# Attention over a memory, then a squared-ReLU MLP: two batches alternate in six pieces instead of four, and each state read runs three batches behind its scores

## The chip, the core and the metric

The kernel runs on one core of a Trainium2 chip. The core has a matrix engine (PE, with its weight loads PEld), a vector engine (DVE), an activation engine (ACT), a general engine (POOL) and a queue engine (SP). Each takes its own instructions in a fixed order, and they meet at semaphores. SP issues nearly all DMAs here, ACT a few. The metric is the time of the program on the device in microseconds (us): before, the median of three runs is 734.01 us (733.97 to 734.39).

## The reference

There are B = 8 batches with H = 8 heads, S = 512 rows of x and N = 32 rows of state per head, each row D = 64 wide. Attention goes both ways between x and state, and the rows of both pass through one MLP:

```python
a  = softmax(x @ state.T / 8);   xread = a  @ state    # 512 rows a batch
a2 = softmax(state @ x.T / 8);   sread = a2 @ x        # 32 rows a batch
rows = concat([xread, sread])    # heads side by side: 544 x 512 a batch
out  = relu(rows @ w_in)**2 @ w_out                    # 512 -> 2048 -> 512
```

Both weight matrices arrive as 8-byte floating point words.

## The kernel before, in words

**Precision.** A matrix product in full precision is made of three products of shortened operands: each operand is cut by `split` (lines 95 to 97) into a high part (a cast on ACT, L96) and a low part (a subtraction on DVE or POOL, L97). The first few products use whole operands instead (`PLAIN_Z`, `PLAIN_X`).

**Weights.** Every weight tile is brought from 8-byte words to single precision by `singles` (L106 to L116): one ACT instruction and four DVE instructions on 128x512. There are 16 tiles of `w_in` (`wf<-w_raw`) and 16 of `w_out` (`wof<-wo_raw`), so 128 such DVE instructions. The converted `w_in` is also stored to DRAM (`wd`), since the second half of the states and the state rows need it again.

**Products with the state.** `xread @ w_in` is never built from `xread`: per head, z = state @ w_in is computed once for a group of four batches (`z_part`, group 0 from the fresh weights, group 1 later from `wd`), copied from PSUM by ACT (`z_stage`, L199) and stored to DRAM (`zd`). `z_fetch` brings the rows of one batch back and splits them (`z_hi`, `z_lo`).

**The units of work.** `mlp` runs over chunks `fc` of 128 of the 2048 hidden columns. A unit is one chunk for one batch: six products into `ph` (the up product, L377), ReLU on ACT (L379), the square (on ACT for the first ten units, then on DVE, L383), the split into `g_hi` (ACT) and `g_lo` (DVE), and twelve products into four accumulators `po` (the down product, L403), two units later. The eight batches have 128 units of 18 products of 128x512; 16 units of 256 columns for the state rows follow at the end. `BOTH` says in which pieces batches 0 and 1 take turns, so that a weight chunk serves two batches while the next is prepared. At the end of a piece the four accumulators are emptied by `rows`.

**Attention.** For each batch and each half of its heads: `scores` (which leaves `e2` and its sum for the state side), `soft1` and `soft1b` (the softmax for the x side, ending in `a_hi`, `a_lo`), and the state read: `load_n`, `cut_n` (split of x, `xn_hl`), `turn` (transposes of `e2` into `e_hl`) and `read` (products `pr`, summed into `sr`).

**What sets the order.** Two lists of steps, `weights` and `reads`, are emitted between units by due times. After that the tile framework's scheduler reorders the instructions of each engine by its own estimates, so the engines' orders have to be read from the built program. They are static: on the chip an instruction that waits holds up all that stands behind it on its engine.

**Buffers.** Tiles of one tag share a number of buffers: `raw` (4) holds weight words, the raw state of group 1 (`st_raw`) and the partial sums on their way back (`so_far`); `x_hl` (1) holds the split x; `xraw` (2) the raw x.

Of the kernel before, what the change touches and what calls it, by code (L numbers as in the profile page):

```python
# [18 lines left out]
def memory_attention_then_relu2_ffn(  # L19
# [19 lines left out]


    nc = tc.nc
    P = 128
# [22 lines left out]
    PLAIN_X = 2  # L65
    BOTH = ((0, 2), (1, 6), (0, NFC), (1, NFC))
    READS = (14, 28)

# [53 lines left out]
    def z_state(G):  # L122
        if G == 0:
            raw = const.tile([P, H, GB * N], F32, name="st_f")
            st["raw"] = raw
        else:
            raw = sb.tile([P, H, GB * N], F32, name="st_raw", tag="raw", bufs=RAW)
        src = stT.rearrange("d (h b n) -> d h b n", h=H, b=B)[:, :, G * GB:(G + 1) * GB, :]
        for j in range(2):
            nc.sync.dma_start(  # L130
                out=raw[j * D:(j + 1) * D].rearrange("d h (b n) -> d h b n", b=GB), in_=src
            )
        hi = sb.tile([P, H, GB * N], F32R, name="stz_hi", bufs=1)
        lo = sb.tile([P, H, GB * N], F32R, name="stz_lo", bufs=1)
        split(hi, lo, raw, nc.gpsimd)
        st[G] = hi, lo

    def z_part(G, k, g):
# [36 lines left out]
        def product(i):  # L175
            def run():
# [65 lines left out]
    def attention_group(b, g, pair):  # L242
# [25 lines left out]
        def scores():  # L268
# [96 lines left out]

    def mlp(width, fcs, first, rows, aux, at_end=None):

# [39 lines left out]
        for i in range(len(fcs) + 2):  # L407
            if i <= last:
                up(fcs[i])
                aux()  # L410
            elif i == last + 1 and at_end:
                at_end()
            if i >= 2:
# [7 lines left out]

    def moved(t, po):
        os_ = sb.tile([P, DM], F32, name="os_", bufs=3)
        if t % 2:
            nc.scalar.copy(out=os_, in_=po)
        else:
            nc.vector.tensor_copy(out=os_, in_=po)
        return os_

# [75 lines left out]
    def order(b):  # L505
        _, pad, (p, q) = attentions[b]
        if b == 1:
            return [
                pad, p["load_t"], p["cut_t"], q["load_t"], p["scores"], p["soft1"], q["cut_t"],
                q["scores"], p["soft1b"], q["soft1"], q["soft1b"],  # L510
            ]
        return [
            pad, p["load_t"], p["cut_t"], q["load_t"], p["scores"], p["soft1"], q["cut_t"],
            p["soft1b"], p["load_n"], q["scores"], q["soft1"], p["turn"], p["cut_n"], q["load_n"],
            q["soft1b"], p["read"], q["cut_n"], q["turn"], q["read"],
        ]
# [17 lines left out]
    for m in range(NFC):  # L534
# [10 lines left out]
        weights.add(steps, 2 * min(at[m], at[m - m % FPC] - 2))  # L545
    weights.add([lambda: z_state(1), z1[0][0], z1[0][2], z1[1][0]], 2 * ends[0] + 4, 2 * ends[0])
    for m in range(NFC):
# [3 lines left out]
        if m + 2 < NFC:  # L551
            steps.append(z1[m + 2][0])
        due = 2 * (ends[0] + (begins[GB] - ends[0]) * (m + 1) // (NFC + 1))
        weights.add(steps, due, 2 * ends[0])
# [10 lines left out]

    half_sums = {}
    for b, fcs in parts:
# [16 lines left out]

        whole = fcs[0] == 0
        so_far = []

        def fetch(b=b, so_far=so_far):
            for t in range(0, NT, 2):
                so_far.append(sb.tile([P, 2, DM], F32, name="so_far", tag="raw", bufs=RAW))  # L590
                nc.sync.dma_start(out=so_far[-1], in_=half_sums[b][:, t:t + 2, :])

        def rows(t, po, b=b, fcs=fcs, so_far=so_far):
            if so_far:
                total = so_far[t // 2][:, t % 2, :]
                nc.vector.tensor_add(out=total, in0=total, in1=po)
            else:
                total = moved(t, po)
            if fcs[-1] < NFC - 1:
                if t == 0:  # L600
                    half_sums[b] = dr.tile([P, NT, DM], F32, name=f"half_{b}_{fcs[0]}")
                nc.sync.dma_start(out=half_sums[b][:, t, :], in_=total)
            else:
                nc.sync.dma_start(out=out[b * R + t * P:b * R + (t + 1) * P, :], in_=total)

        mlp(S, fcs, first, rows, aux, None if whole else fetch)


# [24 lines left out]
    def rows(t, po):  # L633
        tile_ = moved(t, po)
        dst = out.rearrange("(b r) e -> b r e", r=R)[t * GB:(t + 1) * GB, S:R, :]
# [36 lines left out]
```

## Time and profile before

| what | value |
|---|---|
| median of 3 runs | 734.01 us (733.97 to 734.39) |
| the profiled execution's own time | 734.09 us |
| its span, first to last instruction | 732.3 us |
| what lies around the span | 1.8 us |
| PE busy | 684.3 us (93%) |
| DVE busy | 480.5 us (66%) |
| ACT busy | 400.8 us (55%) |
| POOL busy | 229.8 us (31%) |
| moved by DMA | 94.71 MB, 129 GB/s over the span |
| granted PE clock, mean | 0.959 |

The span is the time from the first to the last instruction; the execution's own time has 1.8 us more. Shares over the whole span hide the stages: in the first quarter DVE is at nine tenths and more while PE has gaps, afterwards PE is full. A table by windows of time shows both.

### The profile page before, as it was taken

To read this page: it belongs to the slowest core of one execution; us is meant where nothing else is said; L and a number is where in the kernel's file an instruction comes from. 1 tells how busy PE (TensorE), PEld (TensorE's weight loads), DVE (VectorE), ACT (ScalarE), POOL (GpSimd) and SP (SyncE) were. 2 spreads that over 40 slices of the span, in tenths; PEclk is the share of its full clock that TensorE was granted. 3 is DMA by queue.
4 is the path that set the end of the run, shared out by engine and by line. 5 is a ranking of instruction groups with operands and counts; after the bars stand their busy time and mean duration, and the time that the engine had idled before them with its cause. 6 is when DMAs were issued, how large, how long until landed. Compare 5 with 4: busy or idle time off the path is not lost.

```text
span 732.3 us, 9282 instructions
## 1 busy us (share of the span) xinstructions
PE 684.3 (93%) x3112; PEld 554.6 (76%) x3112; DVE 480.5 (66%) x777; ACT 400.8 (55%) x720; POOL 229.8 (31%) x198
## 2 busy tenths in 40 slices
PE   4978887988999999999999999999999999999994
PEld 1545765766788888878887888888888888888893
DVE  4997999984577496438859688486444445433542
ACT  3667786665587587567546555465333334333441
POOL 2455554556367455432432421421110000000000
PEclk9577988998999999999999999999999999999998
DMA  9879788765543844444212431230021112000420
GB/s 260 272 250 303 258 274 264 216 180 164 179 148 114 248 145 146 132 170 142 90 59 81 141 91 34 86 115 30 29 71 46 35 36 86 30 15 0 144 59 29
DMA packets 74163, 94.71 MB, mean 129 GB/s; under 512 B 3972, under 2 KB 55940, under 8 KB 74116
## 3 DMA queue, kind: packets, MB, share of 16 engines
q1 hardware_dynamic: 56708, 77.34, 33.8%
q10 hardware_dynamic: 17408, 16.78, 6.8%
q8 instruction: 24, 0.39, 0.2%
q14 instruction: 23, 0.19, 0.1%
HBM read 62.13 MB, written 31.98 MB: 129 GB/s over the span
## 4 chain that ended last, share of the span: by engine, by line
PE 75%; DVE 12%; ACT 5%; issue 3%; DMA 3%; SPq 0%; ACTq 0%; DVEq 0%
PE po L403 44%; PE ph L377 24%; PE pr L340 2%; DMA st_f<-stT 1%; DVE wof L112 1%; PE pq L274 1%; DVE wof L107 1%; PE pz L182 1%; DVE z_lo L97 1%; DVE wf L112 1%; DVE wof L116 1%; PE pz L190 1%; PE pz L189 1%; DVE g_lo L97 1%; DVE sp_hl L235 1%
## 5 line engine op out<-in xcount | busy, mean ns | idle before, releaser
L403 PE MATMUL po<-wo_hi,g_hi 128*128 128x512 f32 x544 | 218.8, 404 | 11.3 <-ACT g_hi L96 10.5
L403 PE MATMUL po<-wo_lo,g_hi 128*128 128x512 f32 x544 | 217.9, 402 | 0.0
L383 DVE TENSOR_TENSOR ph<-ph,r 128x512 f32<-128x512 f32 (+1 forms) x134 | 89.1, 665 | 150.8 <-ACT r L379 150.3
L379 ACT ACTIVATE r<-ph 128x512 f32<-128x512 f32 (+1 forms) x144 | 82.5, 574 | 167.8 <-PE ph L377 167.2
L403 PE MATMUL po<-wo_hi,g_lo 128*128 128x512 f32 x544 | 157.0, 400 | 1.4 <-DVE g_lo L97 1.1
L403 PEld LDWEIGHTS po<-wo_hi,g_hi 128*128 128x128 f32 x544 | 104.2, 192 | 36.3 <-ACT g_hi L96 13.2
L97 DVE TENSOR_TENSOR g_lo<-ph,g_hi 128x512 fp32r<-128x512 f32 (+1 forms) x144 | 94.5, 656 | 45.6 <-ACT g_hi L96 36.3
L403 PEld LDWEIGHTS po<-wo_lo,g_hi 128*128 128x128 f32 x544 | 105.0, 193 | 23.1 <-POOL wo_lo L97 0.7
L403 PEld LDWEIGHTS po<-wo_hi,g_lo 128*128 128x128 f32 x544 | 103.0, 192 | 23.4 <-DVE g_lo L97 1.5
L96 ACT CAST g_hi<-ph 128x512 fp32r<-128x512 f32 (+1 forms) x144 | 81.1, 563 | 48.0 <-DVE ph L383 35.5
L377 PE MATMUL ph<-a_hi,z_hi 128*128 128x512 f32 x256 | 83.1, 406 | 6.2 <-DVE g_lo L97 4.8
L171 POOL TENSOR_TENSOR w<-wf,w 64x512 fp32r<-64x512 f32 x52 | 72.4, 1392 | 50.7 <-ACT w L170 34.7
L377 PE MATMUL ph<-a_hi,z_lo 128*128 128x512 f32 x256 | 81.4, 399 | 0.0
L377 PE MATMUL ph<-a_lo,z_hi 128*128 128x512 f32 x256 | 81.1, 396 | 0.0
L97 POOL TENSOR_TENSOR xn_hl<-xn_raw,xn_hl 128x1024 fp32r<-128x1024 f32 x16 | 39.1, 2445 | 94.8 <-ACT xn_hl L96 87.3
L377 PEld LDWEIGHTS ph<-a_hi,z_hi 128*128 128x128 f32 x256 | 47.8, 193 | 18.6 <-DVE g_lo L97 6.5
L377 PEld LDWEIGHTS ph<-a_hi,z_lo 128*128 128x128 f32 x256 | 49.4, 193 | 11.1
L377 PEld LDWEIGHTS ph<-a_lo,z_hi 128*128 128x128 f32 x256 | 48.8, 191 | 11.1
L97 DVE TENSOR_TENSOR z_lo<-z_raw,z_hi 128x512 fp32r<-128x512 f32 x64 | 54.4, 850 | 2.1 <-ACT z_hi L96 2.1
L97 POOL TENSOR_TENSOR xt_hl<-xt_raw,xt_hl 128x1024 fp32r<-128x1024 f32 x12 | 29.2, 2437 | 65.5 <-ACT xt_hl L96 41.0
L96 ACT CAST z_hi<-z_raw 128x512 fp32r<-128x512 f32 x64 | 39.4, 616 | 8.0 <-DMA z_raw<-zd 7.6
L199 ACT COPY z_stage<-pz 128x512 f32<-128x512 f32 x64 | 37.1, 585 | 6.4 <-PE pz L190 4.8
(124 smaller groups left out, 836.0 us busy)
## 6 DMA issues: line engine op xcount, KB each, us to landing
zd<-z_stage ACTq DMA_DIRECT2D x64, 256.0 KB
z_raw<-zd SPq DMA_DIRECT2D x63, 256.0 KB
xt_raw<-xT SPq DMA_DIRECT2D x16, 512.0 KB
w_raw<-w_in SPq DMA_DIRECT2D x16, 512.0 KB
wo_raw<-w_out SPq DMA_DIRECT2D x16, 512.0 KB
xn_raw<-xn SPq DMA_DIRECT2D x16, 512.0 KB
wd<-wf SPq DMA_DIRECT2D x16, 256.0 KB
wf<-wd SPq DMA_DIRECT2D x16, 256.0 KB
```

The source lines that it names most:

```text
L96: nc.scalar.copy(out=hi, in_=src)
L97: eng_lo.tensor_sub(out=lo, in0=src, in1=hi.bitcast(F32))
L107: nc.vector.tensor_scalar_max(out_f, out_f, 2.0**-15)
L112: nc.vector.scalar_tensor_tensor(out=bits, in0=high, scalar=-0x40000000, in1=bits, op0=ALU.bitwise_and, op1=ALU.bitwise_or,)
L116: nc.vector.scalar_tensor_tensor(out=bits, in0=low, scalar=29, in1=bits, op0=ALU.logical_shift_right, op1=ALU.bitwise_or,)
L171: nc.gpsimd.tensor_sub(out=w[other], in0=wf[own], in1=w[own].bitcast(F32))
L199: nc.scalar.copy(out=stage, in_=pz)
L340: nc.tensor.matmul(pr[:, q].rearrange("p i c -> p (i c)"), lhsT=my["e"][:, t, q].rearrange("p i n -> p (i n)"), rhs=my["xn"][:, t, q].rear ...
L377: nc.tensor.matmul(ph, lhsT=w, rhs=v, start=i == 0, stop=i == len(todo) - 1)
L379: nc.scalar.activation(r, ph, AF.Relu)
L383: nc.vector.tensor_mul(out=ph, in0=ph, in1=r)
L403: nc.tensor.matmul(po[t], lhsT=g, rhs=w, start=i == 0 and j == 0, stop=i == last and j == 2)
```

## The change

1. `BOTH` has six pieces. Batch 0 now takes chunks 0-1, 2-9 and 10-15, batch 1 takes 0-5, 6-9 and 10-15. Numbered from 0, the units of batch 0 are 0-1, 8-15 and 20-25, those of batch 1 are 2-7, 16-19 and 26-31 (before: 0-1 and 8-21; 2-7 and 22-31). Due times of the weights follow: chunks 10 to 15 are first needed at units 20 to 25, before at 16 to 21.
2. The partial sums no longer go to DRAM (`half_...`: 8 stores of 256 KB, 4 loads of 512 KB). Each batch has a tile `sum` of 128x4x512 in SBUF; the first piece moves its accumulators there (two on ACT, two on DVE), later pieces add to it on DVE, eight additions more in all.
3. Room for it: `st_f` shares the buffer of `x_hl`, `z_stage` has three buffers instead of four, `os_` goes into `raw`.
4. The steps of a state read (`order_read`) are listed with the scores of the batch three later; the reads of batches 5, 6 and 7 are due at 10, 20 and 30 slots into batch 7 (two slots a unit). `e2` and `s2` have six buffers instead of four.
5. The work on state group 1 is due between units 32 and 64, before between 22 and 64.

```diff
-    BOTH = ((0, 2), (1, 6), (0, NFC), (1, NFC))
-    READS = (14, 28)
+    BOTH = ((0, 2), (1, 6), (0, 10), (1, 10), (0, NFC), (1, NFC))
+    LATE = 3
...
-            raw = const.tile([P, H, GB * N], F32, name="st_f")
+            raw = sb.tile([P, H, GB * N], F32, name="st_f", tag="x_hl", bufs=1)
...
-                stage = sb.tile([P, nq, FW], F32, name="z_stage", bufs=4)
+                stage = sb.tile([P, nq, FW], F32, name="z_stage", bufs=3)
...
-            e2 = sb.tile([P, S], F32, name="e2", bufs=4)
-            s2 = sb.tile([P, 1], F32, name="s2", bufs=4)
+            e2 = sb.tile([P, S], F32, name="e2", bufs=2 * LATE)
+            s2 = sb.tile([P, 1], F32, name="s2", bufs=2 * LATE)
...
-    weights.add([lambda: z_state(1), z1[0][0], z1[0][2], z1[1][0]], 2 * ends[0] + 4, 2 * ends[0])
+    z1_from = begins[GB - 2]
+    weights.add([lambda: z_state(1), z1[0][0], z1[0][2], z1[1][0]], 2 * z1_from + 4, 2 * z1_from)
...
-    reads.add(order(1), 2 * begins[1] - 1)
-    for i in (1, 2):
-        reads.add(order_read(i - 1), 2 * READS[0] + i * (READS[1] - READS[0]), 2 * READS[0])
-    for b in range(2, B):
-        reads.add(order(b), 2 * begins[b] - 1, 2 * ends[b - 2])
+    for b in range(1, B + LATE):
+        steps = order_read(b - LATE) if b >= LATE else []
+        if b < B:
+            steps += order(b)
+            reads.add(steps, 2 * begins[b] - 1, 2 * ends[b - 2] if b > 1 else 0)
+        else:
+            reads.add(steps, 2 * begins[B - 1] + 10 * (b - B + 1))
...
-            if so_far:
-                total = so_far[t // 2][:, t % 2, :]
-                nc.vector.tensor_add(out=total, in0=total, in1=po)
+            if fcs[0] == 0:
+                if t == 0:
+                    sums[b] = sb.tile([P, NT, DM], F32, name="sum", bufs=2)
+                move(t, sums[b][:, t, :], po)
             else:
...
+                nc.vector.tensor_add(out=sums[b][:, t, :], in0=sums[b][:, t, :], in1=po)
+            if fcs[-1] == NFC - 1:
+                nc.sync.dma_start(
+                    out=out[b * R + t * P:b * R + (t + 1) * P, :], in_=sums[b][:, t, :]
+                )
```

**What the scheduler makes of it: the end of the weight conversions on DVE.** The last of the 128 conversion instructions is the last `wof<-wo_raw,wof` row here. Before, DVE's order is (lines one lower than after the change):

```order
L116 SCALAR_TENSOR_TENSOR wof<-wo_raw,wof 128x512
L107 TENSOR_SCALAR wof<-wof 128x512
L97 TENSOR_TENSOR g_lo<-ph,g_hi 128x512
L108 TENSOR_SCALAR wof<-wof 128x512
L112 SCALAR_TENSOR_TENSOR wof<-wo_raw,wof 128x512
L116 SCALAR_TENSOR_TENSOR wof<-wo_raw,wof 128x512
L383 TENSOR_TENSOR ph<-ph,r 128x512
L347 TENSOR_REDUCE both<-pr 128x256
L97 TENSOR_TENSOR e_hl<-pt,e_hl 128x8x64
L97 TENSOR_TENSOR g_lo<-ph,g_hi 128x512
L97 TENSOR_TENSOR z_lo<-z_raw,z_hi 128x512
```

and with the change:

```order
L117 SCALAR_TENSOR_TENSOR wof<-wo_raw,wof 128x512
L108 TENSOR_SCALAR wof<-wof 128x512
L281 TENSOR_TENSOR st<-pq,st_low 64x512
L109 TENSOR_SCALAR wof<-wof 128x512
L98 TENSOR_TENSOR g_lo<-ph,g_hi 128x512
L113 SCALAR_TENSOR_TENSOR wof<-wo_raw,wof 128x512
L384 TENSOR_TENSOR ph<-ph,r 128x512
L281 TENSOR_TENSOR st<-pq,st_low 64x512
L117 SCALAR_TENSOR_TENSOR wof<-wo_raw,wof 128x512
L290 STREAM_TRANSPOSE q_1727<-st 128x512
L292 TENSOR_REDUCE nm_1729<-st 128x1
L98 TENSOR_TENSOR g_lo<-ph,g_hi 128x512
```

Ahead of the last conversion 17 `g_lo` instructions stood, one a unit; now there are 14. The state read (`both`, `e_hl`) has left this place, and the scores of batch 2 (`st`, then a transpose and a reduction) have come to it; before, its `st` rows stood between the 24th and the 29th `g_lo`. Counted over DVE's order up to the last conversion, 7 `ph` rows became 5, 10 `z_lo` rows became 9, two `e_hl` and one `both` went, two `st` rows came, and the rest is the same.

**The raw state of group 1.** It is loaded by SP (`st_raw`) and cast by ACT (`stz_hi`). SP before:

```order
L213 DMA z_raw<-zd_6_97 128x2x256
L433 DMA wo_raw<-w_out 128x1024
L147 DMA wf<-wd_83 128x512
L591 DMA so_far<-half_0_447 128x1024
L147 DMA wf<-wd_84 128x512
L256 DMA xn_raw<-xn 128x4x256
L591 DMA so_far<-half_0_447 128x1024
L130 DMA st_raw<-stT 64x8x128 x2
L147 DMA wf<-wd_84 128x512
L213 DMA z_raw<-zd_7_98 128x2x256
```

SP now:

```order
L430 DMA wo_raw<-w_out 128x1024
L157 DMA wd_90<-wf 128x512
L430 DMA wo_raw<-w_out 128x1024
L148 DMA wf<-wd_83 128x512
L430 DMA wo_raw<-w_out 128x1024
L148 DMA wf<-wd_83 128x512
L131 DMA st_raw<-stT 64x8x128
L214 DMA z_raw<-zd_4_95 128x2x256
L131 DMA st_raw<-stT 64x8x128
L610 DMA wi_raw<-wd_83 128x4x128
```

ACT before:

```order
L106 ACTIVATE wof<-wo_raw 128x512
L96 CAST g_hi<-ph 128x512
L201 DMA zd_7_98<-z_stage 128x2x256
L96 CAST wo_hi_1293<-wof 128x512
L379 ACTIVATE r<-ph 128x512
L96 CAST stz_hi<-st_raw 128x1024
L96 CAST xn_hl<-xn_raw 128x8x128
L96 CAST wo_hi_1293<-wof 128x512
L96 CAST e_hl<-pt 128x8x64
L96 CAST g_hi<-ph 128x512
```

ACT now:

```order
L107 ACTIVATE wof<-wo_raw 128x512
L97 CAST wo_hi_1162<-wof 128x512
L202 DMA zd_7_98<-z_stage 128x2x256
L380 ACTIVATE r<-ph 128x512
L97 CAST z_hi<-z_raw 128x512
L200 COPY z_stage<-pz 128x512
L97 CAST stz_hi<-st_raw 128x1024
L171 CAST w_1_1990<-wf 64x512
L107 ACTIVATE wof<-wo_raw 128x512
L280 COPY st_low<-pq 64x512
L202 DMA zd_7_98<-z_stage 128x2x256
L97 CAST g_hi<-ph 128x512
```

The load stood behind two loads of partial sums (`so_far`) and one of x; now it follows the last `w_out` load, with one `z_raw` load between its two halves. The cast stood behind the last `w_out` activation and now stands one before it.

More of the change, by code (lines that the diff above doesn't have):

```diff
@@ L363, in attention_group, with mlp @@
         return {f.__name__: f for f in names}
-    def mlp(width, fcs, first, rows, aux, at_end=None):
+    def mlp(width, fcs, first, rows, aux):
         nt = width // P
@@ L564, in aux @@
         slot[0] += 1
-    half_sums = {}
+    sums = {}
     for b, fcs in parts:
@@ L583, in first, with rows @@
             ]
[L585 to L593, printed above, removed]
-            if so_far:
-                total = so_far[t // 2][:, t % 2, :]
-                nc.vector.tensor_add(out=total, in0=total, in1=po)
-            else:
[L598 to L606, printed above, removed]
+        def rows(t, po, b=b, fcs=fcs):
+            if fcs[0] == 0:
+                if t == 0:
+                    sums[b] = sb.tile([P, NT, DM], F32, name="sum", bufs=2)
+                move(t, sums[b][:, t, :], po)
+            else:
+                nc.vector.tensor_add(out=sums[b][:, t, :], in0=sums[b][:, t, :], in1=po)
[3 more added lines that the diff above has]
+                )
+        mlp(S, fcs, first, rows, aux)
+    while reads.done < len(reads.steps):
+        reads.next()
     NS = B * N
```

25 lines of the change are left out of this document (8 added, 17 removed).

## The prediction

> **What bounds the kernel now.** I read the page's slices first, then a table of windows, then DVE's groups and waits in the one bad stretch.
>
> ```profile
> span 732.3 us, 9282 instructions
> PE   4978887988999999999999999999999999999994
> DVE  4997999984577496438859688486444445433542
> PEclk9577988998999999999999999999999999999998
> ```
>
> Only the first ten or so of the 40 slices have a PE below 9 tenths, and there DVE stands at 9. In windows of time (us; busy us and count of each engine; granted clock, DMA share, GB/s):
>
> ```profile
> 20.00:163.00 143.00, 122.69 (x473) 91.42 (x474) 135.71 (x199) 98.61 (x182) 77.48 (x56) 0.85 0.79 252
> 163.00:190.00 27.00, 23.09 (x99) 18.66 (x98) 13.40 (x20) 13.79 (x22) 12.96 (x13) 0.87 0.48 133
> 190.00:650.00 460.00, 457.25 (x2121) 377.66 (x2120) 288.08 (x479) 253.39 (x443) 132.41 (x120) 1.00 0.31 99
> 720.00:732.30 12.30, 2.12 (x10) 1.40 (x8) 1.12 (x2) 0.85 (x2) 0.00 (x0) 0.76 0.14 43
> 570.00:580.00 10.00, 10.00 (x45) 8.21 (x44) 4.07 (x6) 2.97 (x6) 0.00 (x0) 1.00 0.09 29
> ```
>
> The last 10 us are the last copies and stores, which stay. From 190 to 720 PE is full: a product of 128x512 every 0.222 us (10 us / 45), so a unit of 18 takes 4.0 us. Whatever the other engines get or lose there is hidden as long as PE keeps its queue. Between 20 and 163 us DVE works 135.7 of 143 us and PE, at a mean clock of 0.85, finishes only some 17 units. That stretch sets the kernel's loss. Its DVE groups and all of DVE's waits:
>
> ```profile
> L116 DVE SCALAR_TENSOR_TENSOR wof<-wo_raw,wof 128x512 int32<-128x512 int32 x16 | 15.8, 989 | 0.1
> L97 DVE TENSOR_TENSOR g_lo<-ph,g_hi 128x512 fp32r<-128x512 f32 x17 | 11.6, 682 | 3.4 <-ACT g_hi L96 3.4
> L97 DVE TENSOR_TENSOR z_lo<-z_raw,z_hi 128x512 fp32r<-128x512 f32 x10 | 10.4, 1042 | 0.0
> L383 DVE TENSOR_TENSOR ph<-ph,r 128x512 f32<-128x512 f32 x8 | 5.5, 689 | 0.7 <-ACT r L379 0.7
> L97 DVE TENSOR_TENSOR e_hl<-pt,e_hl 128x512 fp32r<-128x512 f32 x2 | 1.4, 680 | 0.0
> L347 DVE TENSOR_REDUCE both<-pr 128x256 f32<-128x512 f32 x1 | 0.7, 679 | 0.0
> ...
> DVE g_lo L97 <- ACT g_hi L96: 3.4, 4, 1.9
> DVE wf L107 <- ACT wf L106: 1.8, 1, 1.8
> DVE ph L383 <- ACT r L379: 0.7, 1, 0.7
> DVE wof L107 <- ACT wof L106: 0.4, 1, 0.4
> ```
>
> So DVE waits for 6.3 us in all, never for a DMA directly: it is bound by its own work, mostly the 128 conversions, and since its order is static, PE's units come out at the places where their `g_lo` stands between the conversions. The stretch ends with the last conversion, and a stall follows:
>
> ```profile
> 162.01 0.69 DVE L116 SCALAR_TENSOR_TENSOR wof<-wo_raw,wof 128x512 int32<-128x512 int32 x1
> 162.62 0.69 DVE L383 TENSOR_TENSOR ph<-ph,r 128x512 f32<-128x512 f32 x1
> 163.87 1.04 ACT L96 CAST stz_hi<-st_raw 128x1024 fp32r<-128x1024 f32 x1 [3.85 <-DMA st_raw<-stT]
> 167.40 0.79 PE L403 MATMUL po<-wo_hi,g_hi 128*128 128x512 f32 x1 [3.91 <-ACT g_hi L96]
> ...
> 160.00:170.00 10.00, 6.09 (x22) 4.64 (x21) 5.41 (x8) 4.41 (x8) 5.97 (x4) 0.84 0.81 192
> 170.00:180.00 10.00, 10.00 (x44) 8.15 (x44) 6.21 (x9) 5.55 (x10) 5.61 (x8) 0.82 0.43 134
> ```
>
> ACT waits 3.85 us for `st_raw`, `g_hi` stands behind it, PE idles 3.91 us, and the clock falls: (1 - 0.84) x 10 + (1 - 0.82) x 10 = 3.4 us of it lost. Together the stall costs about 7 us. DVE's own time is over at 162.7 us (162.01 + 0.69).
>
> **The change, part by part.** I take the moment of the last conversion as the mark, and ask when it comes, how much PE then still owes, and what is lost after it.
>
> *When it comes.* By the order of DVE shown above, 3 `g_lo` (0.682), 2 squares `ph` (0.689), 1 `z_lo` (1.042), 2 `e_hl` (0.680) and 1 `both` (0.679) no longer stand ahead of it: 2.05 + 1.38 + 1.04 + 1.36 + 0.68 = 6.5 us less. Two `st` of batch 2 do (0.680 in the row below): 1.4 us more. The conversions and both batches' softmax are the same. The mark moves from 162.7 to 157.6: **-5.2 us**.
>
> *What PE still owes.* Three units fewer are done: counted over PE's order up to the next up product that may follow, 18 `ph` and 32 `po` less, 50 x 0.222 = 11.1 us; 16 `pr` of half width (0.111) and 12 transposes (taken as 0.1, between a quarter and a half of 0.222), 1.8 + 1.2, have moved behind; 8 `pq` (1.8) have come before. PE owes 11.1 + 3.0 - 1.8 = **+12.3 us** more at a mark that comes 5.2 us sooner. Though the weights' due times are later, the scheduler has put more conversions in front of each unit.
>
> *The stall behind the mark.* `st_raw` no longer stands behind `so_far`, and no wait at the cast is left if it lands in time; its second half stands behind a `z_raw`. Gain 0 to 7.0 us; I take **-6**, as only one load is left ahead of it.
>
> *DVE behind the mark.* Before, reads and units stood here; now the scores of batch 2 and the additions at the end of a piece (after unit 15) stand between four `g_lo`. From a window where DVE is not pressed:
>
> ```profile
> L280 DVE TENSOR_TENSOR st<-pq,st_low 64x512 f32<-64x512 f32 x23 | 15.6, 680 | 4.9 <-ACT st_low L279 4.4
> L289 DVE STREAM_TRANSPOSE q<-st 128x512 f32<-128x512 f32 x12 | 8.5, 711 | 0.4
> L97 DVE TENSOR_TENSOR z_lo<-z_raw,z_hi 128x512 fp32r<-128x512 f32 x49 | 39.4, 805 | 0.6 <-ACT z_hi L96 0.6
> L235 DVE SCALAR_TENSOR_TENSOR sp_hl<-sp_raw,sp_hl 64x128 fp32r<-64x128 f32 x10 | 7.7, 774 | 0.2
> L325 DVE TENSOR_SCALAR e<-e,s 128x512 f32<-128x512 f32 x12 | 6.3, 529 | 0.0
> L596 DVE TENSOR_TENSOR so_far<-so_far,po 128x512 f32<-128x512 f32 x4 | 2.6, 682 | 4.3 <-PE po L403 4.3
> ```
>
> Up to the fourth `g_lo` there are 4 `g_lo` and 4 `ph` (5.5), 2 `z_lo` (1.6), 2 `st` (1.4), 8 transposes and reductions like L289, `e_hl` with them (5.6 at about 0.70), 2 `e` (1.1), 2 `sp_hl` of L235 and their 2 halves (taken as 2.4 together), 4 additions (2.7) and small ones (about 1): 21.3 us. PE in the same stretch has 50 products of 512 (11.1), 16 `pz` and 8 `pr` of half width (2.7) and 4 transposes (0.4): 14.2 us. DVE is the later by up to 7.1 us. Its instructions start a little before the one ahead has ended (162.62 against 162.01 + 0.69 = 162.70, 0.08 us), which over some 42 of them takes 3.4 us off: 3.7. The bounds are 0 and +7.1, and I take **+4**.
>
> *DVE's waits ahead of the mark.* With units further back in its order, their inputs are ready when their turn comes, and SP's queue loses the stores and loads of partial sums that weight loads stood behind:
>
> ```profile
> SPq L591 <- DVE wof L116: 7.7, 3, 4.2
> SPq L602 <- DVE wof L107: 1.6, 1, 1.6
> ```
>
> Of the 6.3 us of waits between none and all may go: 0 to -6.3. Since most of them are the chain through `g_hi` on ACT, which stays, I take **-2**.
>
> *Ends of pieces.* Two more, after units 15 and 19. Two rows show what an end can cost:
>
> ```profile
> 92.50 0.80 PE L403 MATMUL po<-wo_hi,g_hi 128*128 128x512 f32 x1 [2.80 <-ACT g_hi L96]
> 189.22 2.56 DVE L596 TENSOR_TENSOR so_far<-so_far,po 128x512 f32<-128x512 f32 x4 [1.34 <-PE po L403]
> ```
>
> When DVE lags, PE finds nothing else to do and idles, 2.80 us near the end after unit 7; when PE is the bound, as at 189 us, nothing: it releases the additions and goes on. 0 to +5.6; taken at **0**, the additions being in DVE's sum already.
>
> *Hidden or free.* 4 additions after unit 19 (2.7 us), the two early reads, and the denser work on group 1 lie in a PE-bound stretch where DVE has 460.0 - 288.1 = 172 us free; if that cover failed, they would cost some 2.7 + 2 x 2.7 = 8 us. 4.2 MB of partial sums leave the queues, cover: DVE. `z_stage` with three buffers can hold up ACT by a store's landing; the nearest row is ACT's 3.85 us for `st_raw`, so 0 to +3.9; in DVE's stretch ACT works 98.6 of 143 us and has time to spare, and I take 0. `st_f` in the buffer of `x_hl` makes the cast of batch 2's x wait for the last whole product; it stands behind that product's copy on ACT anyway: 0.
>
> Conversions and POOL interfere, in this trace: the same operation L108 takes 0.43 us alone and 1.48 us while POOL works.
>
> ```profile
> 8.93 0.43 DVE L108 TENSOR_SCALAR wf<-wf 128x512 int32<-128x512 int32 x1
> 28.36 1.64 POOL L97 TENSOR_TENSOR a_lo<-at,a_hi 128x512 fp32r<-128x512 f32 x1 [0.37 <-ACT a_hi L96]
> 28.80 1.48 DVE L108 TENSOR_SCALAR wf<-wf 128x512 int32<-128x512 int32 x1
> ...
> L97 POOL TENSOR_TENSOR xn_hl<-xn_raw,xn_hl 128x1024 fp32r<-128x1024 f32 x2 | 4.8, 2420 | 5.4 <-ACT xn_hl L96 5.4
> L356 POOL TENSOR_TENSOR sr<-both,low 32x64 f32<-32x64 f32 x4 | 2.0, 498 | 0.2
> ```
>
> Two `xn_hl` and four `sr` leave the stretch and two `xt_hl` of the same 128x1024 come, so my sum has nothing for it. The Trainium skill (SBUF — State Buffer, "Who interferes with whom") says that such DVE instructions and GpSimd take turns on a shared port pair, the later one blocked until the other ends; these rows agree. By it the 2.0 us of the `sr` additions at most would come back to DVE, and the sum would be up to 2 us lower.
>
> **Sum:** -5.2 + 12.3 - 6 + 4 - 2 + 0 = +3.1 us on the span of 732.3: 735.4. The execution's time has 1.8 us more (734.09 against 732.3) and stands 0.1 above the median of 734.01, so 737.2, rounded to **737**.
>
> **Rivals.** (1) *DVE stops waiting.* If weight loads that no longer queue behind partial sums, and units that find their inputs ready, take all of DVE's 6.3 us away, and the scores behind the mark fit under PE (0 instead of +4), with the whole stall gone: -5.2 + 12.3 - 7 + 0 - 6.3 = -6.2, or 728. With the other terms as taken it decides from a mark earlier than 151 us: my sum has the mark at 157.6 - 2 = 155.6, and 4.6 us more turn +3.1 into -1.5. For it: `so_far` and `half` do hold up SP. Against: DVE waited little. (2) *Balance*: the two halves of the sum cancel, 733 to 735. The sum's bounds are wide enough for that. (3) *Piece ends under a lagging DVE*: both cost 2.80 us of PE, 737.2 + 5.6 = 743. For it: the end after unit 15 lies right behind the mark. (4) *DMA bounds the stretch*: 4.2 MB less at 252 GB/s is 16.6 us, so 717. For it: a DMA share of 0.79; against: DVE's waits of 6.3 us are all on ACT, and 135.7 us of its own work do not shrink with the transfers. The page SBUF — State Buffer ("A bandwidth-pool intuition that's wrong") of the Trainium skill holds that HBM is almost always the end-to-end bottleneck. That speaks for rival 4; the rows of DVE do not agree.
>
> **How the numbers follow.** Forecast (slower, 735.6 to 741): 0.40. Rival 3: 0.08. Rival 2: 0.20. Rival 1: 0.27. Rival 4: 0.05. A measurement here can tell about 0.2% (1.5 us) from no change. So slower 0.48, same 0.20, faster 0.32. The range goes down to rival 1 with a little more and up to rival 3: **727 to 744**.
>
> **What would show it.** Right: the last `wof` conversion ends near 156 us with 14 `g_lo` done; PE's idle and half clock grow between 70 and 150 us; no ACT wait for `st_raw` of 3 us or more; DVE above 9 tenths from the mark to about 177 us; PE full from 190 us on. Wrong: a mark before 151 us; waits at the piece ends of 2 us; or idle PE after 200 us, which would mean that the late reads or group 1 lost their cover.

## The result

The changed kernel takes **742.4 us** (median of 4 runs, 741.03 to 743.51) beside 734.2 us for the kernel before on the same chip (733.97 to 736.53): a ratio of **1.0113, 95% interval 1.0094 to 1.0133**. The profiled execution took 741.03 us with a span of 739.0 us, 6.7 us more than before. The ratios below rest on fast runs: one of the ten runs of a kernel further down (`after_reads`) took 1127.84 us at a granted clock of 0.557 and is left out of its ratio.

Span and slices of the page of the changed kernel:

```profile
span 739.0 us, 9276 instructions
PE   5963597888999999999999999999999999999994
DVE  5999899999649844446845695979654445443542
PEclk8776899899999999999999999999999999999998
```

PE's weak slices are the same first ten as before. Four of them are weaker, above all the fourth and the fifth (about 55 to 92 us), which have 3 and 5 tenths where they had 8 and 8; the prediction had expected the loss from 70 to 150 us. DVE stands at 9 in nearly all of them. The same windows as before (busy us and count of PE, PEld, DVE, ACT, POOL; clock, DMA share, GB/s):

```profile
20.00:163.00 143.00, 103.51 (x394) 75.55 (x393) 138.89 (x184) 95.83 (x174) 77.49 (x52) 0.82 0.74 230
163.00:190.00 27.00, 24.97 (x112) 20.18 (x111) 24.76 (x45) 18.66 (x34) 14.79 (x11) 0.92 0.39 125
```

From 20 to 163 us PE issues 394 products instead of 473, while DVE is busy for 3.2 us more with 15 instructions fewer (184 for 199). POOL's busy time is the same to 0.01 us. So DVE's instructions became dearer. The groups of its conversions in that stretch (count | busy us, mean ns of one | idle before them):

```profile
L117 DVE SCALAR_TENSOR_TENSOR wof<-wo_raw,wof 128x512 int32<-128x512 int32 x16 | 18.9, 1184 | 0.1
L113 DVE SCALAR_TENSOR_TENSOR wof<-wo_raw,wof 128x512 int32<-128x512 int32 x16 | 18.9, 1180 | 0.3
L113 DVE SCALAR_TENSOR_TENSOR wf<-w_raw,wf 128x512 int32<-128x512 int32 x14 | 16.3, 1166 | 0.2
L109 DVE TENSOR_SCALAR wof<-wof 128x512 int32<-128x512 int32 x16 | 14.0, 878 | 0.3
L117 DVE SCALAR_TENSOR_TENSOR wf<-w_raw,wf 128x512 int32<-128x512 int32 x14 | 13.1, 938 | 0.1
L108 DVE TENSOR_SCALAR wf<-wf 128x512 f32<-128x512 f32 x14 | 11.5, 818 | 1.5 <-ACT wf L107 1.5
L109 DVE TENSOR_SCALAR wf<-wf 128x512 int32<-128x512 int32 x14 | 9.3, 666 | 0.2
L108 DVE TENSOR_SCALAR wof<-wof 128x512 f32<-128x512 f32 x16 | 8.8, 550 | 1.0 <-ACT wof L107 1.0
```

All of DVE's waits there (us in total, times, longest):

```profile
DVE wf L108 <- ACT wf L107: 1.5, 1, 1.5
DVE wof L108 <- ACT wof L107: 1.0, 2, 0.8
DVE s L308 <- ACT q L303: 0.3, 1, 0.3
```

The eight groups add up to 110.8 us; the same 120 instructions took 100.8 us before (the eight groups of that trace: 15.8, 14.8, 14.4, 13.2, 12.9, 10.9, 10.9, 7.9). The growth is in the instructions with two tile operands; beside the row of the prediction these are the others before:

```profile
L112 DVE SCALAR_TENSOR_TENSOR wof<-wo_raw,wof 128x512 int32<-128x512 int32 x16 | 14.4, 899 | 0.1
L112 DVE SCALAR_TENSOR_TENSOR wf<-w_raw,wf 128x512 int32<-128x512 int32 x14 | 13.2, 946 | 0.0
L116 DVE SCALAR_TENSOR_TENSOR wf<-w_raw,wf 128x512 int32<-128x512 int32 x14 | 12.9, 925 | 0.1
```

These four groups took 56.3 us before and take 67.2 now; the four TENSOR_SCALAR groups took 44.5 and take 43.6. DVE's waits fell from 6.3 to 2.8 us. DVE's timeline around 134 us, with POOL's instructions, shows what makes a conversion dear:

```profile
133.82 2.70 POOL L172 TENSOR_TENSOR w<-wf,w 64x512 fp32r<-64x512 f32 x2 [1.33 <-issue]
133.89 1.49 DVE L109 TENSOR_SCALAR wof<-wof 128x512 int32<-128x512 int32 x1
135.30 0.68 DVE L98 TENSOR_TENSOR g_lo<-ph,g_hi 128x512 fp32r<-128x512 f32 x1
137.11 0.69 DVE L117 SCALAR_TENSOR_TENSOR wof<-wo_raw,wof 128x512 int32<-128x512 int32 x1
138.17 0.43 DVE L109 TENSOR_SCALAR wof<-wof 128x512 int32<-128x512 int32 x1
138.59 1.28 POOL L98 TENSOR_TENSOR wo_lo<-wof,wo_hi 128x512 fp32r<-128x512 f32 x1 [2.07 <-ACT wo_hi L97]
138.63 1.79 DVE L113 SCALAR_TENSOR_TENSOR wof<-wo_raw,wof 128x512 int32<-128x512 int32 x1
```

L109 takes 0.43 us alone and 1.49 beside POOL; the other form (L113, L117) 0.69 and 1.79; `g_lo`, which reads one operand from PSUM, keeps its 0.68 beside POOL. What PE waits for from 20 to 163 us shows where the time goes ahead of the last conversion. These are the two groups with the longest single waits in the changed kernel, then the same two before:

```profile
PE pz L190 <- POOL w L172: 8.7, 2, 8.4
PE po L404 <- ACT g_hi L97: 7.6, 3, 7.2
```

```profile
PE pz L189 <- POOL w L171: 3.5, 1, 3.5
PE po L403 <- ACT g_hi L96: 4.3, 3, 2.8
```

The wait of 8.4 us ends at 71.7 us. POOL's `w` stands behind a cast on ACT, and that cast waits for a conversion of `wf` on DVE. Ahead of it, from 59.3 to 68.2 us, five conversions in a row took 1.38 to 2.58 us each, with POOL at work. The wait of 7.2 us ends at 92.4 us. Ahead of its `g_hi`, ACT had itself waited for weight words:

```profile
86.61 0.66 ACT L107 ACTIVATE wf<-w_raw 128x512 f32<-128x512 f32 x1 [2.98 <-DMA w_raw<-w_in]
```

In this stretch ACT's waits for such loads come to 9.1 us in the changed kernel (3.0 for `w_in`, 6.1 for `w_out`) and to none before. So DVE is not alone in the loss ahead of the mark; how much the later loads took was not separated.

The last conversion in DVE's timeline, the three `g_lo` behind it and the dearest row between them:

```profile
161.40 1.44 DVE L117 SCALAR_TENSOR_TENSOR wof<-wo_raw,wof 128x512 int32<-128x512 int32 x1
163.95 0.67 DVE L98 TENSOR_TENSOR g_lo<-ph,g_hi 128x512 fp32r<-128x512 f32 x1
166.88 0.67 DVE L98 TENSOR_TENSOR g_lo<-ph,g_hi 128x512 fp32r<-128x512 f32 x1
169.03 2.69 DVE L236 SCALAR_TENSOR_TENSOR sp_hl<-sp_raw,sp_hl 64x128 fp32r<-64x128 f32 x2
176.97 0.68 DVE L98 TENSOR_TENSOR g_lo<-ph,g_hi 128x512 fp32r<-128x512 f32 x1
```

PE's waits from 158 to 190 us:

```profile
PE ph L378 <- DVE g_lo L98: 3.1, 1, 3.1
PE po L404 <- DVE sum L585: 2.0, 1, 2.0
```

The mark lies at 161.40 + 1.44 = 162.84 us, nearly where it was (162.70). Ten microseconds pass between the 16th and the 17th `g_lo`, filled with the softmax of batch 2, `sp_hl` and additions at the end of a piece, and PE waits for `g_lo` and for those additions.

**A measure for all kernels below.** "Lost time" at a unit is the start of its first `ph` product less the time of all products ahead of it in PE's order, each at the distance between starts that PE shows where it is full (0.229 us for 128x512 in `ph` and `po`, 0.12 or less for half width and transposes). It doesn't depend on how much other work stands ahead of the unit. At the end it is taken at the last product. Since some short products take less than their fixed distance, a value can fall along a row, by up to 2.4 us. Each row is one profiled execution, up to 1.6 us from the median of its kernel, so differences of that size between rows are not read.

| kernel | `g_lo` ahead of the last conversion | that conversion starts | lost at unit 11 | unit 17 | unit 20 | unit 24 | end |
|---|---|---|---|---|---|---|---|
| before | 17 | 162.0 | 54.1 | 60.5 | 67.7 | 69.0 | 73.5 |
| changed | 14 | 161.4 | 67.1 | 75.4 | 79.8 | 79.7 | 80.2 |
| before, raw states shared | 15 | 161.4 | 62.5 | 68.2 | 68.3 | 69.5 | 73.1 |
| before, six pieces | 19 | 168.4 | 52.7 | 57.9 | 59.5 | 59.8 | 72.3 |
| before, late reads | 17 | 157.4 | 52.7 | 58.2 | 66.4 | 66.3 | 66.4 |
| late reads, six pieces | 19 | 170.4 | 54.4 | 57.1 | 63.8 | 63.6 | 68.6 |
| changed, group 1 from batch 0's end | 14 | 160.3 | 67.7 | 74.9 | 74.8 | 76.2 | 74.2 |
| changed, scores held | 14 | 160.6 | 68.2 | 74.2 | 74.1 | 74.0 | 75.2 |
| changed, reads of before | 14 | 162.3 | 68.3 | 72.9 | 72.9 | 72.7 | 70.5 |
| raw states apart, reads two later | 16 | 162.4 | 56.1 | 65.2 | 65.9 | 66.0 | 69.7 |

The difference at the end, 80.2 - 73.5 = 6.7 us, is that of the spans. By unit 8 the changed kernel has already lost 10 us more than the kernel before (56.6 against 46.7).

### The profile page after: what moved, and what is told of

The parts are those of the page before. It is cut to its first block, busy times and chain, and to the rows that moved or that the text cites. A ratio compares the mean times of both kernels' runs of the same rounds, so it can differ in the third digit from the quotient of the medians.

```text
span 739.0 us, 9276 instructions
## 1 busy us (share of the span) xinstructions
PE 677.0 (92%) x3112; PEld 551.9 (75%) x3112; DVE 494.9 (67%) x785; ACT 400.8 (54%) x720; POOL 229.2 (31%) x198
## 2 busy tenths in 40 slices
DMA packets 72435, 90.51 MB, mean 122 GB/s; under 512 B 3780, under 2 KB 55748, under 8 KB 72388
## 4 chain that ended last, share of the span: by engine, by line
PE 72%; DVE 16%; DMA 5%; issue 3%; ACT 1%; SPq 0%; POOL 0%; ACTq 0%; DVEq 0%; POOLq 0%
PE po L404 43%; PE ph L378 23%; DMA wo_raw<-w_out 3%; PE pr L341 2%; DVE wof L113 2%; DVE wof L117 2%; DVE wf L113 2%; DMA st_f<-stT 1%; DVE wf L108 1%; DVE wof L109 1%; PE pq L275 1%; DVE z_lo L98 1%; DVE g_lo L98 1%; PE pz L191 1%; PE pz L190 1%
## 5 line engine op out<-in xcount | busy, mean ns | idle before, releaser
L404 PE MATMUL po<-wo_hi,g_hi 128*128 128x512 f32 x544 | 217.8, 402 | 12.9 <-ACT g_hi L97 8.2
L404 PE MATMUL po<-wo_lo,g_hi 128*128 128x512 f32 x544 | 215.1, 396 | 0.1
L384 DVE TENSOR_TENSOR ph<-ph,r 128x512 f32<-128x512 f32 (+1 forms) x134 | 88.9, 663 | 168.6 <-ACT r L380 168.4
L404 PE MATMUL po<-wo_hi,g_lo 128*128 128x512 f32 x544 | 155.2, 397 | 3.9 <-DVE g_lo L98 3.9
L172 POOL TENSOR_TENSOR w<-wf,w 64x512 fp32r<-64x512 f32 x52 | 72.7, 1398 | 82.7 <-ACT w L171 63.3
```

The lines of the kernel that those rows point to most:

```text
L172: nc.gpsimd.tensor_sub(out=w[other], in0=wf[own], in1=w[own].bitcast(F32))
L384: nc.vector.tensor_mul(out=ph, in0=ph, in1=r)
L404: nc.tensor.matmul(po[t], lhsT=g, rhs=w, start=i == 0 and j == 0, stop=i == last and j == 2)
```

## The experiments

Each time is a median beside that of the kernel before on the same chip; a ratio has its 95% interval.

**1. Conversions held back (after_pin, before_pin).** My first theory: the loss is the order alone, conversions standing too far ahead of units. Every conversion was queued on DVE behind the newest `g_lo` emitted before it:

```diff
     def singles(out_f, words):
+        if len(g_los) > 0:
+            with tc.issue_after(g_los[-1 - 0].ins):
+                singles_(out_f, words)
+        else:
+            singles_(out_f, words)
+
+    def singles_(out_f, words):
...
-            split(hi, lo, ph, nc.vector)
+            g_los.append(split(hi, lo, ph, nc.vector))
```

> The changed kernel, but each weight conversion on DVE is held behind the newest g_lo that was written before it in program order, so that the last conversion stands behind 22 g_lo instead of 14; nothing else is altered. If the place of the conversions in DVE's order sets the loss, the time falls from 742 us to between 715 and 735 (the last conversion comes some 10 us later, near 172, but 8 units = 32 us of PE work are done by then). If the extra piece ends, the late reads or the transfers set it, the time stays within 5 us of 742.

> The kernel before, with the same hold on the conversions: the last one stands behind 19 g_lo instead of 17, and those of the middle are spread more evenly. By the theory of DVE's order a gain, but a smaller one than in the changed kernel: 734 falls to 720 to 732. By the rivals no change (732 to 736).

Measured: changed kernel with it 740.92 us (1.0100, 1.0078 to 1.0121), kernel before with it 757.47 us (1.0318, 1.0295 to 1.0341). The theory in this form fell. The changed kernel held in this way, in the window from 20 to 163 us:

```profile
20.00:163.00 143.00, 105.83 (x411) 78.16 (x410) 112.55 (x180) 89.71 (x166) 60.09 (x43) 0.83 0.66 210
```

The two groups in which PE waits longest there:

```profile
PE po L413 <- ACT g_hi L97: 17.0, 6, 8.9
PE ph L387 <- ACT a_hi L97: 8.4, 1, 8.4
```

DVE is now idle for 30 us of the 143: the engine that bounds the stretch was made to stand still early, and the conversions that it owed came late (the last one at 194.7 us). Lost time is 71.0 us at unit 20 and 79.0 at unit 24. So this run does not show what the order alone costs: a hold that idles DVE costs about as much as it could gain.

**2. Parts of the change alone (before_stf, before_six).**

```diff
-            raw = const.tile([P, H, GB * N], F32, name="st_f")
+            raw = sb.tile([P, H, GB * N], F32, name="st_f", tag="x_hl", bufs=1)
```

> The kernel before with one line of the change alone: st_f shares the buffer of x_hl. The built order then has the last conversion behind 15 g_lo instead of 17, and two more conversions of w_in ahead of the third g_lo, much as in the changed kernel. Theory of DVE's order: slower by 3 to 8 us (737 to 742). If piece ends, late reads or sums in SBUF set the loss: 733 to 736.

```diff
-    BOTH = ((0, 2), (1, 6), (0, NFC), (1, NFC))
+    BOTH = ((0, 2), (1, 6), (0, 10), (1, 10), (0, NFC), (1, NFC))
```

> The kernel before with six pieces alone (sums still through DRAM, reads as before). The last conversion stands behind 18 g_lo, and there are two more piece ends. Theory of DVE's order: 726 to 735, not slower. If the two more piece ends cost PE what one row showed (2.80 us each): 738 to 741.

Measured: 735.33 us (1.0033, 1.0014 to 1.0052) and 733.57 us (1.0014, 0.9996 to 1.0032). The first is what the rival expected. The one line on `st_f` brings a good part of the changed order with it: 15 `g_lo` ahead of the last conversion instead of 17, and 62.5 us lost at unit 11 instead of 54.1; at unit 4 it has lost 47.5 us, the changed kernel 45.9 and the kernel before 41.3. It pays most of that back, since the stall for `st_raw` is gone: the lost time stands at 68.2 to 68.3 from unit 17 to 20, where the kernel before goes from 60.5 to 67.7. Six pieces cost nothing that can be told from no change, two more piece ends included. Two effects hide in that. At unit 20 the lost time is 59.5 us where the kernel before has 67.7, and after unit 24 PE stands still once:

```profile
191.61 1.04 ACT L96 CAST stz_hi<-st_raw 128x1024 fp32r<-128x1024 f32 x1 [7.01 <-DMA st_raw<-stT]
196.64 0.79 PE L403 MATMUL po<-wo_hi,g_hi 128*128 128x512 f32 x1 [5.91 <-ACT g_hi L96]
```

This is the stall of the kernel before, later and longer: `g_hi` stands on ACT behind the cast of `st_raw`. What six pieces give without it is not shown.

**3. POOL's work beside the conversions (after_wwo, before_wwo).** Low halves of group 0's weights and of `w_out` move from POOL to DVE:

```diff
-                nc.gpsimd.tensor_sub(out=w[other], ...)
+                (nc.gpsimd if G else nc.vector).tensor_sub(out=w[other], ...)
...
-        split(wo[k][0][:, i, :], wo[k][1][:, i, :], wf, nc.gpsimd)
+        split(wo[k][0][:, i, :], wo[k][1][:, i, :], wf, nc.vector)
```

> The changed kernel with the low halves of group 0's weights (w, 26 subtractions) and of the second weights (wo_lo, 16) computed on DVE instead of POOL; nothing is left out. In the changed kernel's trace a conversion on DVE takes 0.415 or 0.68 us while POOL rests and 1.31 or 1.51 us while POOL works beside it. Theory (the mark did not move because POOL's work beside the conversions makes them dearer): the conversions between 20 and 163 us fall from 110.8 us to 70 to 80, the 42 subtractions add at most 42 x 0.68 = 29 us to DVE, so that DVE owes about 5 to 10 us less in that stretch and more units are done by the last conversion: 728 to 737 us. Rival (the price of a conversion comes from something else, from the DMAs or from DVE itself): DVE owes up to 29 us more, 750 to 770 us.

> The kernel before with the same 42 subtractions on DVE instead of POOL; nothing is left out. Theory: the conversions between 20 and 163 us fall from 100.8 us to 70 to 80, which pays for the 29 us added within a few us: 726 to 738 us. Rival: 745 to 765 us.

Measured: 739.08 us (1.0084, 1.0059 to 1.0109) and 740.33 us (1.0093, 1.0062 to 1.0125): 2 us above the theory's ranges, 11 and 5 us below the rival's. Groups of DVE from 20 to 163 us in the changed kernel with this edit:

```profile
L109 DVE TENSOR_SCALAR wof<-wof 128x512 int32<-128x512 int32 x14 | 5.9, 419 | 0.1
L113 DVE SCALAR_TENSOR_TENSOR wof<-wo_raw,wof 128x512 int32<-128x512 int32 x14 | 12.7, 910 | 0.1
L113 DVE SCALAR_TENSOR_TENSOR wf<-w_raw,wf 128x512 int32<-128x512 int32 x14 | 9.7, 690 | 0.0
L172 DVE TENSOR_TENSOR w<-wf,w 64x512 fp32r<-64x512 f32 x20 | 14.8, 739 | 0.7
L98 DVE TENSOR_TENSOR wo_lo<-wof,wo_hi 128x512 fp32r<-128x512 f32 x13 | 9.6, 742 | 0.3 <-ACT wo_hi L97 0.3
```

And the last conversion in its timeline:

```profile
191.91 0.68 DVE L117 SCALAR_TENSOR_TENSOR wof<-wo_raw,wof 128x512 int32<-128x512 int32 x1
```

The price is confirmed: with POOL nearly silent (23.6 us busy in the window), L109 on `wof` falls from 878 to 419 ns and L113 on `wf` from 1166 to 690. The conversions there cost 71.6 us for 111 of them, 0.645 each, where the changed kernel has 110.8 for 120, 0.923 each. That is 30.9 us less for 111, against 14.8 + 9.6 = 24.4 us for the 33 subtractions that fall into the window. The gain does not reach the end: lost time is 52.6 us at unit 11 (changed: 67.1), 61.2 at unit 17, then 75.3 at unit 24. In the order built for this kernel the last conversion stands behind the 21st `g_lo`, at 191.9 us, with scores of batch 2 (`st`) among the last conversions; from 158 to 200 us PE waits 6.1 us for `st` and 2.3 for a `g_lo`. So the dear conversions are real, but taking POOL off them does not decide the time; where the mark would lie with the old order and cheap conversions is not shown.

**4. Late reads alone, and all but them (before_late, after_reads).**

```diff
-    READS = (14, 28)
+    LATE = 3
...
+    for b in range(1, B + LATE):
+        steps = order_read(b - LATE) if b >= LATE else []
+        if b < B:
+            steps += order(b)
+            reads.add(steps, 2 * begins[b] - 1, 2 * ends[b - 2] if b > 1 else 0)
+        else:
+            reads.add(steps, 2 * begins[B - 1] + 10 * (b - B + 1))
```

This is the edit of `before_late`, with six buffers for `e2` and `s2` and the read steps taken out of `order`; `after_reads` takes the same lines out of the changed kernel.

> The kernel before with the late reads alone (a state is read three batches after its scores; four pieces, sums through HBM, the raw states in their own buffer). The order of DVE up to the last conversion is that of the kernel before. Theory (the loss comes from the order that goes with the sums and with st_f in the buffer of x_hl, and from the scores of batch 2 pulled forward): 732 to 736 us. Rival (the late reads alone bring the loss): 738 to 743 us.

> The changed kernel with the reads of before (each state is read with its batch's own scores); six pieces and sums in SBUF remain. Up to the last conversion 14 g_lo stand ahead on DVE as in the changed kernel, but the scores of batch 2 no longer stand right behind it; they come some six units later. If the scores behind the mark cost the 4.4 us that were lost there: 736 to 739 us. If DVE's work is only put off and lost later: 741 to 744 us.

Measured: **726.28 us** (0.9905, 0.9878 to 0.9932) and 731.40 us (0.9972, 0.9957 to 0.9987). Both are some 5 us below the lower of the two expectations. Late reads alone make the kernel before 7 us faster (0.95% of 733); in the changed kernel the same lines make it 10 us slower (1.0113 against 0.9972). The stretch in the kernel before with late reads:

```profile
20.00:163.00 143.00, 116.34 (x445) 85.18 (x443) 133.07 (x190) 97.05 (x179) 73.87 (x50) 0.87 0.80 250
```

DVE and POOL both have less to do than before (133.1 for 135.7 us, 73.9 for 77.5), the last conversion starts at 157.4 instead of 162.0 us, and after unit 20 nothing more is lost (66.4 at unit 20 and at the end; before, 67.7 and 73.5). So of the 7.1 us between the two at the end 1.3 are there at unit 20, and 5.8 come after it, where the page shows PE full. In the kernel before, PE has five short waits after 185 us, four of them for `g_hi` on ACT, 2.7 us together; with late reads it has one of 1.4 us. The rest was not traced.

**5. What turns the gain into a loss (after_scpin, after_z1).** In the changed kernel the first transposes of batch 2's scores stand on DVE behind the 14th `g_lo`, right after the last conversion, and behind the 16th (the text on record below counts them one later); with the reads of before, behind the 22nd and 25th. The first edit queues them there. The second gives group 1's weights their old start, so that they are emitted ahead of these scores again:

```diff
+        late = [i for i in range(2) if step in [
+            attentions[2][2][i][n] for n in ("scores", "soft1", "soft1b")]]
+        if late:
+            with tc.issue_after(g_los[21 + 3 * late[0]].ins):
+                step()
+        else:
+            step()
```

> The changed kernel with one thing added: on DVE the instructions of batch 2's scores are queued behind the 22nd and the 25th g_lo, where they stand too when the reads of before are kept; in the changed kernel they stand behind the 15th and the 16th, right behind the last conversion. Nothing is left out. Theory (the late reads and the later start of group 1 empty the queue ahead of these scores, the scheduler pulls them up behind the last conversion, where DVE is behind already, and PE starves there): the loss between units 15 and 20 goes, 730 to 736 us, near the 731.4 us with the reads of before. Rival (DVE's work is the same and is only lost later, or the loss comes from somewhere else in the late reads): 739 to 743 us.

```diff
-    z1_from = begins[GB - 2]
+    z1_from = ends[0]
```

> The changed kernel with group 1's weights begun where batch 0 ends, as before the change (z1_from = ends[0]), so that its products stand ahead of batch 2's scores again; these move to behind the 17th and the 19th g_lo. Nothing is left out. Theory (it is the later start of group 1, together with the late reads, that pulls the scores up): 735 to 740 us. Rival (that start does nothing for the time): 741 to 744 us.

Measured: 735.79 us (1.0043, 1.0029 to 1.0056) and 734.00 us (1.0014, 1.0002 to 1.0026). The first lies in its theory's range, the second 1 us below. In the timeline of DVE with the old start of group 1, the 16th and the 17th `g_lo` and what is between them:

```profile
164.13 0.69 DVE L98 TENSOR_TENSOR g_lo<-ph,g_hi 128x512 fp32r<-128x512 f32 x1 [0.59 <-ACT g_hi L97]
167.55 0.70 DVE L384 TENSOR_TENSOR ph<-ph,r 128x512 f32<-128x512 f32 x1 [2.73 <-ACT r L380]
168.16 0.68 DVE L281 TENSOR_TENSOR st<-pq,st_low 64x512 f32<-64x512 f32 x1
168.90 0.69 DVE L98 TENSOR_TENSOR g_lo<-ph,g_hi 128x512 fp32r<-128x512 f32 x1
```

4.8 us instead of 10.1, and DVE even waits for ACT. Windows of both edits behind the mark, the old start first and the held scores second:

```profile
163.00:190.00 27.00, 26.09 (x123) 21.37 (x121) 22.32 (x37) 16.86 (x31) 12.31 (x8) 1.00 0.40 125
```

```profile
163.00:190.00 27.00, 26.64 (x118) 21.74 (x117) 17.40 (x29) 11.22 (x20) 1.29 (x1) 1.00 0.18 59
```

PE is busy for 26.1 and 26.6 of 27 us at full clock, in the changed kernel 24.97 at 0.92. Up to unit 17 all three have lost the same (74 to 75 us); then the changed kernel goes on to 79.8 and these two stand at 74 to 76. The hold also leaves POOL and the queues nearly idle there (1.29 us busy, 59 GB/s), so it moves more than DVE's order; the old start of group 1 does not, and gains as much. So a late start of group 1 together with late reads lets the scheduler pull batch 2's scores up to the place where DVE is behind already, and that costs 5 us (1.0113 against 1.0043) to 7 us (against 1.0014). How the scheduler comes to this was not looked into.

**6. Back to the parts (late_six, const_two).** The first is the kernel before with late reads and six pieces. The second is the changed kernel with group 1's old start, `st_f` in its own buffer, and `LATE = 2`, which makes the room:

> The kernel before with the late reads and with six pieces; running sums through HBM, the raw states in their own buffer and the start of group 1 as before the change. Nothing is left out. Batch 2's scores stand behind the 28th g_lo. Late reads alone gave 726.3 us, six pieces alone 733.6 us beside 733.2 us. Theory (six pieces cost nothing by themselves, the late reads gain where the scores stay away from the last conversion): 722 to 728 us. Rival (late reads don't go with six pieces): 731 to 742 us.

```diff
-    LATE = 3
+    LATE = 2
...
-            raw = sb.tile([P, H, GB * N], F32, name="st_f", tag="x_hl", bufs=1)
+            raw = const.tile([P, H, GB * N], F32, name="st_f")
...
-    z1_from = begins[GB - 2]
+    z1_from = ends[0]
```

> The changed kernel with group 1's weights begun where batch 0 ends, the raw states in a buffer of their own again, and a state read two batches after its scores instead of three (four buffers for e2 and s2 instead of six, which makes the room). Six pieces and sums in SBUF remain; nothing is left out. On DVE 16 g_lo stand ahead of the last conversion (14 in the changed kernel and with z1_from alone set back, 18 to 19 with late reads and six pieces through HBM). Theory (the 5.5 us between late reads with six pieces through HBM, 728.5 us, and the changed kernel with group 1's start set back, 734.0 us, are the price of st_f's place in the buffer of x_hl, which orders more conversions early): 725 to 731 us. Rival (they are the price of the sums in SBUF, or a state has to be read three batches late): 733 to 738 us.

Measured: 728.54 us (0.9944, 0.9922 to 0.9965) and 728.64 us (0.9938, 0.9921 to 0.9955); the first half a microsecond above its theory's range, the second inside. PE's longest wait from 140 to 200 us in the first is one for a partial sum on its way through HBM:

```profile
PE po L403 <- DVE so_far L592: 4.0, 1, 4.0
```

With sums in SBUF and `st_f` apart, that wait is gone and the units move up, 16 `g_lo` ahead of the last conversion instead of 14, and 56.1 us lost at unit 11 instead of 67.7. Since that kernel also reads two batches late instead of three, it shows the price of `st_f`'s place only together with that.

**The change taken apart.** The parts in a chain, against the kernel before of their own chip: late reads -0.95%; with six pieces -0.56%; with sums in SBUF, `st_f` in the buffer of `x_hl` and three `z_stage` +0.14%; with the late start of group 1 +1.13%. Of 733 us: -7.0, then +2.9, +5.1 and +7.3. Each ratio is uncertain by 0.12 to 0.27 points, so each step by some 2 us, and since the parts act on each other's order, another chain would give other steps (six pieces alone: +0.14%). Of the kernels tried, late reads alone are the fastest: 726.3 us.

## Why the prediction was right or wrong

The direction was right, and 742.4 us lies inside the range, 5 us above the predicted time. The steps hold less well than the sum, and that the total stays in the range is partly luck: a gain of 5.4 us that nothing in the prediction foresaw offsets more than half of its largest miss. In lost time the difference of 6.7 us is 13.2 (73.8 at unit 15 against 60.6 at unit 18, the last units begun before the marks) - 7.1 (the stall that only the kernel before has, units 18 to 20) + 6.0 (changed, units 15 to 20) - 5.4 (from unit 20 to the end: 5.8 before, 0.4 after).

- *When it comes*, -5.2, with DVE's waits another -2: **this step failed.** The mark came at 162.84 us, not near 156. The waits fell by 3.5 us, more than taken, but the conversions cost 10.0 us more. The prediction had seen L108 take 0.43 and 1.48 us and yet counted POOL's instructions one by one, so that "my sum has nothing for it". POOL's busy time did not change; how much of it fell beside conversions did, 53.8 us of the window before and 63.2 now, counted from the two traces. The growth is all in the instructions with two tile operands. By the Trainium skill (SBUF — State Buffer, "Who interferes with whom"), a DVE instruction in a two-port mode contends with GpSimd, one with two SBUF inputs contends with a GpSimd instruction that reads SBUF, and one with at most one SBUF input and no such mode does not. The rows agree: conversions 0.43 to 1.49 us, `g_lo` with one operand from PSUM 0.68 us beside POOL too.
- *What PE still owes*, +12.3: right. 13.2 us at marks 0.1 us apart, with the 14 `g_lo` that were forecast. (A product takes 0.229 us where PE is full, not 0.222: the 45 records counted in 10 us include one cut by the window's edge. Over 50 products that is 0.35 us.)
- *The stall behind the mark*, -6: right, 1 us small. In the changed kernel `st_raw` is cast at 150.6 us, and ACT never waits for it.
- *DVE behind the mark*, +4 within 0 to 7.1: 6.0 us, DVE busy for 24.76 of 27 us. The mechanism was right, the size at the upper half of its bounds.
- *Ends of pieces*, 0: one wait of 2.0 us came, at the end after unit 15, which the prediction had named as a sign against it. It lies within the 6.0 us above; six pieces alone moved nothing in the total that can be told.
- *Hidden or free*, 0: **failed in part.** "the two early reads, and the denser work on group 1" were priced as instructions under a full PE. Late reads alone are worth -7 us in the kernel before. The 5.4 us that the kernel before loses after unit 20 and the changed one doesn't were not foreseen. Late reads alone take them away (66.4 at unit 20 and at the end), but the changed kernel with the reads of before loses nothing there either (72.9 and 70.5), so which part of the change does it stays open. The later start of group 1 costs 7 us once the reads are late; it does so through the scores behind the mark, for which the sum had a term of its own.

By size: the mark's failure took 8.1 us more than the sum had (13.2 against 12.3 - 7.2), the stall gave 1.1 more, DVE behind the mark took 2.0 more, and the end gave 5.4: 3.1 + 8.1 - 1.1 + 2.0 - 5.4 = 6.7.

Rivals: *DVE stops waiting* fell with the mark. *Balance* fell: the ratio's interval lies above 1. *Piece ends* had 743 us, but not by its mechanism: one end cost 2.0 us, not two of 2.8. Its price was misread too: at 92.50 us in the kernel before `g_hi` stands on ACT behind a cast that waited 2.67 us for a conversion, not for an addition. *DMA bounds the stretch* fell: 4.2 MB less were moved (90.51 for 94.71 MB), DMA share 0.74 for 0.79 in the stretch, and the time rose; single loads came late all the same, as ACT's 9.1 us of waits show. The sentence of the Trainium skill that stood behind this rival (SBUF — State Buffer, "A bandwidth-pool intuition that's wrong") doesn't hold for this stretch.

## What to carry to other kernels

Where a scheduler sets the order, price a due time or a shared buffer by what it does to the order of the engine that bounds a stage: which products are still waiting for that engine, and what was put in front of them. When a change makes work of one engine denser, look up what stood between before: an instruction's time in the old trace is a mixture of alone and contended, and the mixture moves. A change with several parts is worth taking apart even when its sum is small: here one part alone was worth -7 us, and another cost 7 us once the rest was in.

## What the runs showed of the hardware

The conversions' dearness beside POOL was visible before; that the mean of 120 instructions could move by 10% with the same instructions and the same busy time on POOL (77.48 and 77.49 us) was not expected. In the changed trace a TENSOR_SCALAR conversion takes 0.415 us where POOL works for less than a tenth of it and 1.31 us where POOL works for more than six tenths (34 and 21 instructions from 20 to 163 us), a SCALAR_TENSOR_TENSOR one 0.68 and 1.51 us (23 and 29). With the subtractions moved, the engine that took on more instructions had less to do: 224 instructions in 127.4 us of the window instead of 184 in 138.9, though with 9 conversions fewer in it.
